# Attention: value products issued in portions of 128 queries, longer planned costs for the filling work, later transfers of the sums

## The chip, the cores and the metric

The kernel runs on one core of a Trainium2 chip. The metric is device time in microseconds. The engines of the core are TensorE (PE, with its weight loads as PEld), VectorE (DVE), ScalarE (ACT), GpSimd (POOL) and SyncE (SP); the last two also issue transfers (DMAs), SP all the loads of operands, POOL those that carry the sums and results of the attention.

## The reference

Four layers follow each other on a sequence of 2048 rows of 640 numbers: attention, state-space convolution, attention, convolution, each on a layer norm of its input and added to it. The change touches the attention alone:

```python
def _A_ref(x, wqkv, wo):
    B, S, D = x.shape                       # 1, 2048, 640
    H, Dh = 32, D // 32                     # 32 heads of 20
    qkv = (x @ wqkv).reshape(B, S, 3, H, Dh).transpose(2, 0, 3, 1, 4)
    q, k, v = qkv[0], qkv[1], qkv[2]
    p = softmax(einsum("bhqd,bhkd->bhqk", q, k) * Dh ** -0.5)
    o = einsum("bhqk,bhkd->bhqd", p, v)
    return o.transpose(0, 2, 1, 3).reshape(B, S, D) @ wo
x = x + _A_ref(layernorm(x), A_wqkv, A_wo)
```

The convolution's kernel is the real part of a sum over 128 modes, `K[d, l] = 2 Re sum_n C[d, n] exp(A[d, n] dt[d] l)`. It does not depend on x, and both convolution layers use the same one.

## The kernel before

**The attention loop.** A layer's 32 heads are taken in 8 groups of 4 (`g`), the 2048 queries in 4 blocks of 512 (`qb`), the keys in 16 tiles of 128 (`kt`), and the four heads of a group in two pairs (`j`). One step of `kt` and `j` is: `scores` multiplies keys and queries (8 matmuls in fp16, line 775, one score group) into one of two PSUM buffers `S`, and ACT takes the exponential of its 128 x 1024 numbers into a tile `pt` (line 778). A layer has 8 x 4 x 16 x 2 = 1024 such steps. After both pairs of a `kt`, `values` multiplies the exponentials with the values (line 792, 8 matmuls in fp32 over 512 queries, which the trace shows as 16 records because each runs in two passes) and sums over `kt` in the PSUM pair `pa`. A row of ones beside the values gives the softmax's denominators.

**The end of a block.** With the last `kt` of a block, DVE copies and adds `pa` into `oc`. The denominators then travel: POOL writes them to DRAM (`sums`: dn<-oc, 4 transfers), reads them back spread over 128 partitions (`load`: dr<-dn), DVE takes the reciprocal (`invert`), POOL writes them (`back`: dn<-dr) and reads them broadcast (`spread`: db<-dn, 4 transfers). At the end of the next block DVE multiplies (`scale`) and POOL stores the block (ot<-oc). The list at line 838 gives the moments, in planned us after the block's end.

**Work that fills TensorE.** Between score groups stands work that later steps need: the projections of queries and keys for the next 128 columns (`qk`, line 560, 15 steps of 8 matmuls for a piece of 512 rows, 8 pieces for a block `b` of columns), the squares of their norms (`norms`, line 488), the projections of values (`values_of`, line 524, 15 matmuls for 128 rows), and in the first layer the convolution's kernel: DVE makes the two factors (tiles `ka`, `kb`), and `contract` (line 314, 16 matmuls a step, two steps for 8 channels) multiplies them. The powers from which DVE starts come by a large load on POOL (kpw<-wd), the finished kernel leaves by kd<-ko.

**What sets the order.** The program is written out by a planner: `plan.pe`, `plan.act` and `plan.dve` are planned clocks, and each piece of work carries a planned cost. `fill`, called after each score group, first places the oldest value product that is ready (`ready`) and then calls `slot` as long as the next step ends 0.5 us before the planned end of the exponential. `slot` takes either a projection step or a `contract` step; `AHEAD` (line 33) says how many us of projections must have been placed by which score group before a `contract` step may go first. `need` forces what a group of heads requires: at `kt` 10 of the last block of a group it places the remaining projections of the next group's columns at once, then `finish` reduces the norms (POOL's k2m), writes the shifts (qm<-mr, 4 transfers), and the loads of the next keys and queries (kop, qop on SP) follow, of which qop<-qm reads the shifts. DVE, POOL's transfers, SP and the matmuls of the loop are tied to the order in which the planner wrote them; other instructions may be moved by the scheduler when they are ready.

`end_jobs`, when all filling work is placed, starts the loads of the output weights (wot), their split on POOL (woh, wol) and, in the first layer, the loads of x (x<-in_x_in). The first tiles of the attention's result are then loaded (otl<-ot) and split on ACT (oh, line 956) between the last exponentials.

Of the kernel before, what the change touches and what calls it, by code (L numbers as in the profile page):

```python
# [21 lines left out]
P = 128  # L22
L = 2048
D = 640
NI = L // P
# [4 lines left out]
NA, NB = 32, 64  # L30
LV = [1.0, 2.0, 4.0, 8.0, 16.0, 32.0, 64.0, 128.0, 256.0, 512.0, 1024.0, 1536.0]
PB = 7
AHEAD = ((0, 0.0), (96, 22.0), (352, 47.0), (478, 72.0), (724, 125.0))
WS = 256.0
LG = 2
BOUND = 30.0
# [4 lines left out]
VP = DH + 1  # L41
VW = VP * 7 + 32
QW = DH * 8
# [38 lines left out]
def mha_s4d_kernel(ctx, tc, x_in, wqkv, wo, lar, aim, cr, ci, ldt, dsk,  # L82
                   c_e1, c_eb, c_f2, c_fa, c_sel, c_lv, c_id, c_sg, c_e16, c_f16, c_id16, out, parts="asas", general=None):
    nc = tc.nc
    plan = Plan()
# [8 lines left out]
    se, te = nc.scalar, nc.tensor  # L94
# [81 lines left out]
    def chain(ins):  # L176
        last[0] = tie(ins, last[0])

    def kgen():
# [124 lines left out]
        def contract(r, bs, sub, ko, a, b):  # L304

            ps = pst("M", [P, 512], F32, tag=f"m{r}", name=f"m{r}")[:, :DC // 4 * NB].rearrange("p (c b) -> p c b", b=NB)
            for c8 in range(DC // 4):
                if c8:
                    yield plan.pe + 0.7, 0.43, True, ()
                plan.on_pe(0.43)  # L310
                for n in range(4):
                    for j in range(4):
                        ch, dd = DC * (sub % 2) + 4 * c8 + j, 4 * c8 + j
                        chain(te.matmul(ps[32 * j:32 * j + 32, c8, :], a[n // 2][:, ch, :], b[n][:, dd, :],  # L314
                                        start=(n == 0), stop=(n == 3), tile_position=(0, 32 * j)))
            evac = lambda: ve.tensor_copy(ko[:, 2 * sub:2 * sub + 2, :], ps)
            emptied(*((None, evac) if r else (evac,)))
            if sub == BC // DC - 1:
                ge.dma_start(kd[bs, :].rearrange("(c j) (a b) -> (j a) c b", j=4, b=NB), ko)
# [49 lines left out]
    part = [None, None]  # L369
# [21 lines left out]
    def attention(x, stats):  # L391
# [121 lines left out]
        def values_of(i, q, ps, w, n):  # L513

            sl = slice(i * P, i * P + P)
            k = 0
            if n == QW:
                plan.on_pe(0.63)
            for ct in range(NCT):
                for a_, m in ((xh, w[0]), (xh, w[1]), (xl, w[0])):  # L520
                    if k == 8 and n == QW:
                        yield 0.0, 0.63, True, ()
                        plan.on_pe(0.63)
                    chain(te.matmul(ps[:, :n], a_[:, ct, sl], m[:, ct, :], start=(k == 0), stop=(k == 14)))  # L524
                    k += 1
            for d in range(n // QW):
                o = Vt[(q + d) % 3][:, i, :VP * 8].rearrange("p (h r) -> p h r", r=VP)[:, :, :DH]
                src = ps[:, d * QW:d * QW + QW].rearrange("p (h r) -> p h r", r=DH)
                if d == 1 or d and i % 2:
                    se.activation(o, src, AF.Copy, scale=1.0 / WS)  # L530
                elif n == QW:
                    evac = lambda: ve.tensor_scalar_mul(o, src, 1.0 / WS)
                    emptied(*((None, evac) if i % 2 else (evac,)))
                else:
                    ve.tensor_scalar_mul(o, src, 1.0 / WS)

        def jobs():
# [40 lines left out]
            def vq(q):  # L578
                make = stage(2 * D + q * QW, QW, "v")
                yield plan.pe + 5.0, 0.0, False, ()  # L580
                w = make()
                t0 = plan.dve
                for i in range(NI):
                    yield t0, 0.63, False, (i % 2,)
                    yield from values_of(i, q, pst("M", [P, 512], F32, tag=f"m{i % 2}", name=f"m{i % 2}"), w, QW)
                have.add(("v", q))

# [35 lines left out]
        def slot(until=None):  # L623

            if head[0] is None:
                head[0] = next(todo[0], None)
            begun = head[0] and head[0][2]
            if pend and part[0] is None and not begun and (head[0] is None or spent[0] >= ahead(len(ends) - 2)):
                t, f, args = pend[0]
                r = free.index(min(free))  # L630
                t = max(t + 0.15, free[r])
                if t <= plan.pe or until is None and head[0] is None:
                    part[:] = f(r, *args), (t, 0.43, True, ())
                    pend.pop(0)
            step = part[1] if part[0] else head[0]
            if step is None:
                return False
            t = max([step[0], *(free[r] for r in step[3])])
            if until and (t > plan.pe or plan.pe + step[1] > until):
                return False  # L640
            plan.on_pe(0.0, t)
            if part[0]:
                part[1] = next(part[0], None)
                if part[1] is None:
                    part[0] = None
            else:
                spent[0] += step[1]
                head[0] = next(todo[0], None)
            return True
# [111 lines left out]
        sums_ = [plan.pe]  # L761
# [19 lines left out]
            ends.append(plan.act)  # L781
            return pt

        def values(qb, g, kt, pts, pa):

            V = Vt[g // 2 % 3]
            plan.on_pe(0.865)
            for r in range(2):
                rows = slice(64 * r, 64 * r + 64)
                for j in range(4):  # L790
                    h = 4 * (g % 2) + j
                    chain(te.matmul(pa[r][32 * j:32 * j + 32, :], V[rows, kt, VP * h:VP * h + 32],  # L792
                                    pts[j // 2][rows, 512 * (j % 2):512 * (j % 2) + 512],
                                    start=(kt == 0), stop=(kt == NI - 1), tile_position=(64 * r, 32 * j)))
            if kt == NI - 1:
                blk = 4 * g + qb
                oc = ev.tile([P, 512], F32, name="oc")
                dr = ev.tile([P, 16], F32, name="dr")
                db = []
                rows = dn[0, blk].rearrange("(j c) f -> j (c f)", j=4)  # L800
                plan.dve = max(plan.dve, plan.pe + 0.25)
                ve.tensor_copy(oc, pa[0])
                ve.tensor_add(oc, oc, pa[1])
                sums_[0] = plan.dve + 0.15
                if scaled:
                    scaled.pop()()

                def sums():
                    for j in range(4):
                        ge.dma_start(rows[j:j + 1, :], oc[32 * j + DH:32 * j + DH + 1, :])  # L810

                def load():
                    ge.dma_start(dr, dn[0, blk])

                def invert():
                    ve.tensor_scalar_max(dr, dr, 1e-30)
                    ve.reciprocal(dr, dr)

                def back():
                    ge.dma_start(dn[1, blk], dr)  # L820

                def spread():
                    rows = dn[1, blk].rearrange("(j c) f -> j (c f)", j=4)
                    db.append(ev.tile([P, 512], F32, bufs=1, name="db"))
                    for j in range(4):
                        ge.dma_start(db[0][32 * j:32 * j + 32, :], rows[j:j + 1, :].to_broadcast([32, 512]))

                def scale():
                    ve.tensor_mul(oc, oc, db[0])
                    later.append((plan.dve + 0.3, store))  # L830
                    later.sort(key=lambda e: e[0])

                def store():
                    for j in range(4):
                        h = 4 * g + j
                        ge.dma_start(ot[h * DH:(h + 1) * DH, 512 * qb:512 * qb + 512], oc[32 * j:32 * j + DH, :])
                later.extend((plan.dve + n, f) for n, f in (
                    (0.2, sums), (5.0, load), (10.0, invert), (11.0, back), (15.5, spread)))
                later.sort(key=lambda e: e[0])
                scaled.append(scale)  # L840

# [22 lines left out]

        def fill(j):

            if ready:
                t = max(ready[0][0] + 0.15, 0.0 if ready[0][3] else sums_[0])
                if t <= plan.pe + 0.1 or j and len(ready) > 2:
                    plan.on_pe(0.0, t)  # L870
                    values(*ready.pop(0)[1:])
            while slot(plan.act - 0.5):
                pass
            drain_later()
            weave()
# [4 lines left out]
        for g in range(H // 4):  # L880
            need((0, 1, 1, 2, 3, 3, 4, 4)[g], ("v", g // 2))
            for qb in range(4):
# [9 lines left out]
                for kt in range(NI):  # L892
                    kc, pts = P * (kt % 8), []
                    for j in range(2):
                        pts.append(scores(kop[j][kt // 8], kc, qop[j][qb % 2]))
                        if j:
                            ready.append((plan.act, qb, g, kt, pts, pa))
                        fill(j)
                    if kt == 2:
                        for j in range(2):  # L900
# [519 lines left out]
```

## Time and profile before

| | us |
|---|---|
| median of 3 runs (2774.07 to 2780.48) | 2777.54 |
| the profiled execution | 2777.71 |
| its span in the profile | 2775.8 |
| ACT busy in the span | 2352.1 |
| PE busy in the span | 2544.2 |
| the exponentials, 2048 of them, ACT busy | 1930.9 |

A row of the profile's groups reads: line, engine, operation, what is written and read, shape, count, then the busy time, the mean ns of one, and the idle time of the engine just before them with what ended it. A row of the time line reads: start and length in us, engine, line, operation, and in brackets the idle time before it and its releaser. The exponentials of the first attention layer run from 111.8 to 1146.2 us of the span, those of the second from 1564.0 to 2545.4 us. Line numbers in these texts are those of the kernel before; line 74 is the helper that records every DVE, POOL and SP operation, so those are told apart by their tiles.

### The profile page before, as it was taken

The page shows a single profiled execution, that of the slowest core. Times are in us where ns is not written, and L with a number is a line of the kernel's source. Part 1 is how long each engine was busy: PE and PEld are TensorE (multiplying, and loading weights), DVE is VectorE, ACT ScalarE, POOL GpSimd, SP SyncE. Part 2 cuts the span into 40 slices and gives each one's busy share as a digit, 9 for nine tenths or more (in the row PEclk, how much of TensorE's full clock was granted, in tenths as well). Part 3 has the DMA queues.
Part 4 walks back from the last instruction along what each step waited for, and adds up shares of the span by engine and source line. Part 5 has one row for each costly group of instructions (what it writes and reads, how often), then busy time and mean ns, then how long its engine had stood idle before and what let it go on. Part 6 is the DMA issues. An engine that isn't in the chain of part 4 may idle for free.

```text
span 2775.8 us, 117573 instructions
## 1 busy us (share of the span) xinstructions
PE 2544.2 (92%) x51968; PEld 1436.6 (52%) x51968; DVE 1469.0 (53%) x3292; ACT 2352.1 (85%) x2781; POOL 821.2 (30%) x1232
## 2 busy tenths in 40 slices
PE   7898989999999997899999998999999888878998
PEld 3453544444444442587796544544444333335988
DVE  8645778978887870366777333332222100002865
ACT  8797989999999998645665698999999999997464
POOL 1112222323223324300573022222322422222376
PEclk9999999999999999999999999999999999999999
DMA  6512232323222223354543112111211211112365
GB/s 230 162 43 68 54 77 52 85 59 78 56 68 55 57 84 96 100 202 179 198 150 92 34 49 66 54 52 51 55 50 38 69 27 38 39 40 71 106 194 159
DMA packets 179128, 238.65 MB, mean 86 GB/s; under 512 B 36144, under 2 KB 124208, under 8 KB 176816
## 3 DMA queue, kind: packets, MB, share of 16 engines
q1 hardware_dynamic: 143168, 184.44, 20.6%
q0 software_dynamic: 35440, 46.58, 7.8%
q8 instruction: 410, 6.72, 1.0%
q14 instruction: 110, 0.90, 0.1%
HBM read 154.87 MB, written 76.03 MB: 83 GB/s over the span
## 4 chain that ended last, share of the span: by engine, by line
ACT 46%; PE 28%; issue 11%; DVE 7%; DMA 6%; POOL 1%; SPq 0%; ACTq 0%; DVEq 0%; POOLq 0%
ACT pt L778 46%; PE pa L792 4%; PE S L775 3%; PE psv L1148 3%; PE po L1054 3%; PE psy L1158 2%; PE psx L1136 2%; PE psx L1113 2%; PE po L1048 1%; DMA kop<-ks 1%; PE m L314 1%; PE pv L524 1%; PE pst L1123 1%; PE m L560 1%; PE pq L681 1%
## 5 line engine op out<-in xcount | busy, mean ns | idle before, releaser
L778 ACT ACTIVATE pt<-S 128x1024 f32<-128x1024 f32 x2048 | 1930.9, 1041 | 71.8 <-PE S L775 57.2
L792 PE MATMUL pa<-pt,V 64*32 64x512 f32 x16384 | 1099.6, 594 | 0.6 <-DVE oc L74 0.6
L775 PE MATMUL S<-qop,kop 61*32 61x512 f16 x16384 | 869.4, 383 | 160.6 <-ACT pt L778 138.0
L775 PEld LDWEIGHTS <-kop 61*32 61x32 f16 x16384 | 369.9, 90 | 830.7 <-issue 726.1
L74 POOL DMA_DIRECT2D dn<-oc x256 | 125.2, 496 | 835.6 <-DVE oc L74 768.2
L792 PEld LDWEIGHTS pa<-pt,V 64*32 64x32 f32 x16384 | 308.9, 107 | 69.4 <-issue 8.3
L74 DVE COPY oc<-pa 128x512 f32<-128x512 f32 x64 | 44.2, 691 | 414.8 <-PE pa L792 414.7
L74 DVE TENSOR_SCALAR qc<-m 128x512 f32<-128x512 f32 x64 | 44.1, 689 | 289.2 <-PE m L560 289.2
L74 POOL DMA_DIRECT2D db<-dn x256 | 129.3, 511 | 139.7 <-DMA dn<-dr 137.0
L74 DVE TENSOR_TENSOR kb<-ktab 128x512 f32<-128x512 f32 x240 | 155.3, 684 | 1.5 <-PE m L314 1.5
L560 PE MATMUL m<-xh,wh 64*32 64x512 f16 x2560 | 139.1, 380 | 3.0 <-DVE qc L74 3.0
L560 PE MATMUL m<-xh,wl 64*32 64x512 f16 x2560 | 138.3, 378 | 0.7 <-issue 0.7
L560 PE MATMUL m<-xl,wh 64*32 64x512 f16 x2560 | 138.4, 378 | 0.0
L74 POOL DMA_DIRECT2D ot<-oc x256 | 130.7, 517 | 8.9 <-DVE oc L74 6.0
L314 PEld LDWEIGHTS m<-kb,ka 128*32 128x32 f32 x5120 | 79.8, 110 | 101.6 <-issue 64.5
L560 PEld LDWEIGHTS <-wh 64*32 64x32 f16 x5120 | 87.7, 94 | 75.4 <-issue 37.6
L1141 POOL TENSOR_TENSOR t<-t,kb 128x512 f32<-128x512 f32 x80 | 102.1, 1276 | 70.3 <-DVE t L74 69.4
L1125 ACT COPY xt<-pst 128x1024 f16<-128x1024 f16 x80 | 81.6, 1023 | 46.7 <-PE pst L1123 46.5
L314 PE MATMUL m<-kb,ka 128*32 128x64 f32 x5120 | 105.8, 224 | 11.4 <-DVE qc L74 11.4
L74 POOL DMA_DIRECT2D dn<-dr x64 | 35.7, 557 | 234.1 <-DVE dr L74 229.8
L1142 POOL TENSOR_TENSOR t<-t,t 128x512 f32<-128x512 f32 x78 | 99.3, 1273 | 7.3 <-DVE t L74 1.3
L970 POOL TENSOR_TENSOR ul<-u,uh 128x640 f16<-128x640 f32 x30 | 46.5, 1566 | 177.7 <-ACT uh L969 177.7
(273 smaller groups left out, 3770.4 us busy)
## 6 DMA issues: line engine op xcount, KB each, us to landing
ka<-kha SPq DMA_DIRECT2D x80, 256.0 KB
kb<-khb SPq DMA_DIRECT2D x80, 256.0 KB
db<-dn POOLq DMA_DIRECT2D x256, 64.0 KB, 2.8
kpw<-wd POOLq DMA_DIRECT2D x20, 576.0 KB, 7.7
qop<-qs SPq DMA_DIRECT2D x256, 40.0 KB
kop<-ks SPq DMA_DIRECT2D x128, 80.0 KB
ot<-oc POOLq DMA_DIRECT2D x256, 40.0 KB, 2.6
otl<-ot SPq DMA_DIRECT2D x32, 320.0 KB
```

What stands on the lines that cost most here:

```text
L74: made = f(out, *a, **k)
L314: chain(te.matmul(ps[32 * j:32 * j + 32, c8, :], a[n // 2][:, ch, :], b[n][:, dd, :], start=(n == 0), stop=(n == 3), tile_position=(0, 32 ...
L560: chain(te.matmul(ps[r][32 * t:32 * t + 32, :], a_[rows, ct, 32 * t:32 * t + 32], m[rows, ct, sl], start=(k == 0), stop=(k == 14), tile_po ...
L775: chain(te.matmul(S[32 * t:32 * t + 32, 512 * r:512 * r + 512], kt_[rows, kc + 32 * t:kc + 32 * t + 32], qt[rows, :], start=True, stop=Tru ...
L778: se.activation(pt, S, AF.Exp, scale=SCALE)
L792: chain(te.matmul(pa[r][32 * j:32 * j + 32, :], V[rows, kt, VP * h:VP * h + 32], pts[j // 2][rows, 512 * (j % 2):512 * (j % 2) + 512], sta ...
L1054: te.matmul(pos[hf], oh[:, ct, :], m[:, ct, 320 * hf:320 * hf + 320], start=False, stop=(ct == NCT - 1 and m is wol))
L1113: te.matmul(ps[:, r, i, :], e1[:, e, s, r, :], m[:, s, bs], start=(n == 0), stop=(n == 2))
L1125: se.copy(xt, pt.rearrange("p k g c -> p k (g c)"))
L1141: ge.tensor_mul(t2, t2, kb)
L1142: (ge if g0 else ve).tensor_add(t1, t1, t2)
L1148: te.matmul(pv[:, g].rearrange("p r i c -> p (r i c)"), t1[:, g * P:g * P + P], fa, start=True, stop=True)
```

## The change

The value products of a `kt` are cut into four portions of 128 queries, each a unit of its own in `ready`. `values` takes the portion's number, starts the sum with the first portion of the first `kt`, and runs the block's end with the last portion of the last. `fill` places portions by two rules: while more than 8 wait they are placed whatever the plan says, and otherwise only if one is ready and ends 0.5 us before the planned end of the exponential; more than three waiting go ahead of the filling work, the others behind it.

The planned cost of a `contract` step goes from 0.43 to 0.56 us; a value projection is cut into three pieces of 5 matmuls planned at 0.4 us (before: pieces of 8 and 7 at 0.63). The moments of the sums' transfers go from 5, 10, 11 and 15.5 to 6, 14, 14.5 and 20 planned us. `AHEAD` gets other numbers.

```diff
-AHEAD = ((0, 0.0), (96, 22.0), (352, 47.0), (478, 72.0), (724, 125.0))
+AHEAD = ((0, 0.0), (84, 20.0), (340, 44.0), (466, 68.0), (730, 122.0))
...
-                    yield plan.pe + 0.7, 0.43, True, ()
-                plan.on_pe(0.43)
+                    yield plan.pe + 0.7, 0.56, True, ()
+                plan.on_pe(0.56)
...
-                plan.on_pe(0.63)
+                plan.on_pe(0.4)
...
-                    if k == 8 and n == QW:
-                        yield 0.0, 0.63, True, ()
-                        plan.on_pe(0.63)
+                    if k % 5 == 0 and k and n == QW:
+                        yield 0.0, 0.4, True, ()
+                        plan.on_pe(0.4)
...
-        def values(qb, g, kt, pts, pa):
+        def values(part, qb, g, kt, pts, pa):
...
-            plan.on_pe(0.865)
+            plan.on_pe(0.217)
...
-                    h = 4 * (g % 2) + j
-                    chain(te.matmul(pa[r][32 * j:32 * j + 32, :], V[rows, kt, VP * h:VP * h + 32],
-                                    pts[j // 2][rows, 512 * (j % 2):512 * (j % 2) + 512],
-                                    start=(kt == 0), stop=(kt == NI - 1), tile_position=(64 * r, 32 * j)))
-            if kt == NI - 1:
+                    h, c0 = 4 * (g % 2) + j, P * part
+                    chain(te.matmul(pa[r][32 * j:32 * j + 32, c0:c0 + P], V[rows, kt, VP * h:VP * h + 32],
+                                    pts[j // 2][rows, 512 * (j % 2) + c0:512 * (j % 2) + c0 + P],
+                                    start=(kt == part == 0), stop=(part == 3 and kt == NI - 1), tile_position=(64 * r, 32 * j)))
+            if part == 3 and kt == NI - 1:
...
-                    (0.2, sums), (5.0, load), (10.0, invert), (11.0, back), (15.5, spread)))
+                    (0.2, sums), (6.0, load), (14.0, invert), (14.5, back), (20.0, spread)))
...
-            if ready:
-                t = max(ready[0][0] + 0.15, 0.0 if ready[0][3] else sums_[0])
-                if t <= plan.pe + 0.1 or j and len(ready) > 2:
-                    plan.on_pe(0.0, t)
-                    values(*ready.pop(0)[1:])
+            def quarter(late):
+                if not ready:
+                    return False
+                t = max(ready[0][0] + 0.15, 0.0 if ready[0][4] else sums_[0])
+                if not late and (t > plan.pe + 0.1 or plan.pe + 0.22 > plan.act - 0.5):
+                    return False
+                plan.on_pe(0.0, t)
+                values(*ready.pop(0)[1:])
+                return True
+            while len(ready) > 8:
+                quarter(True)
+            while len(ready) > 3 and quarter(False):
+                pass
             while slot(plan.act - 0.5):
                 pass
+            while quarter(False):
+                pass
...
-                            ready.append((plan.act, qb, g, kt, pts, pa))
+                            ready.extend((plan.act, n, qb, g, kt, pts, pa) for n in range(4))
```

Three places show what moves. The first is on PE, in the first block of the first attention layer. `S` is the score group's buffer, `pa` the sum of value products, `m` a projection's. The program of before:

```order
L775 MATMUL S<-qop_107,kop_103 32x512
L792 MATMUL pa_1249<-pt,V_92 32x512 x4
L792 MATMUL pa_1250<-pt,V_92 32x512 x4
L775 LDWEIGHTS kop_101
L775 MATMUL S<-qop_105,kop_101 32x512
...
L560 LDWEIGHTS wh
L560 MATMUL m_1290<-xl,wh 32x512
```

The changed program at the same place:

```order
L775 MATMUL S<-qop_107,kop_103 32x512
L792 MATMUL pa_1249<-pt,V_92 32x128 x4
L792 MATMUL pa_1250<-pt,V_92 32x128 x4
...
L775 LDWEIGHTS kop_101
L775 MATMUL S<-qop_105,kop_101 32x512
...
L792 MATMUL pa_1249<-pt,V_92 32x128 x4
L792 MATMUL pa_1250<-pt,V_92 32x128 x4
L560 LDWEIGHTS wh
L560 MATMUL m_1290<-xl,wh 32x512
```

Three portions now stand between the two score groups where the whole product stood (the pair of rows three times), and the fourth behind the second group, ahead of the projections.

The second place is on POOL, at the start of the second group of heads of the first layer. The program of before, from the shifts of the first `need` on:

```order
L74 DMA qm<-mr 6x512 x4
L74 DMA kd<-ko 128x8x64
L74 DMA dn<-oc 16x1x32 x4
L74 DMA ot<-oc 20x512 x4
L74 DMA kpw_166<-wd 128x36x32
L74 DMA dr<-dn 128x16
L74 DMA dn<-dr 128x16
L74 DMA db<-dn 32x512 x4
```

The changed program:

```order
L74 DMA qm<-mr 6x512 x4
L74 DMA db<-dn 32x512 x4
L74 DMA kd<-ko 128x8x64
L74 DMA kpw_166<-wd 128x36x32
L74 DMA dn<-oc 16x1x32 x4
L74 DMA ot<-oc 20x512 x4
L74 DMA dr<-dn 128x16
L74 DMA dn<-dr 128x16
L74 DMA db<-dn 32x512 x4
```

The large load kpw no longer stands between the stores of the sums and the load dr that reads them back; it is ahead of both.

The third place is on POOL, at the end of the sixth group of heads of the first layer, around the last reduction of norms (`ISA k2m`). The program of before:

```order
L74 DMA dn<-oc 16x1x32 x4
L74 DMA ot<-oc 20x512 x4
L74 ISA k2m<-k_21327 128x2
L74 DMA dr<-dn 128x16
L74 DMA kpw_166<-wd 128x36x32
L74 DMA qm<-mr 7x512 x4
L74 DMA dn<-dr 128x16
```

The changed program:

```order
L74 DMA dn<-oc 16x1x32 x4
L74 DMA ot<-oc 20x512 x4
L74 DMA dr<-dn 128x16
L74 DMA kd<-ko 128x8x64
L74 DMA dn<-dr 128x16
L74 DMA kpw_165<-wd 128x36x32
L74 ISA k2m<-k_30411 128x2
L74 DMA qm<-mr 7x512 x4
```

The reduction and the shifts have moved from the block's beginning to behind the block's other transfers; on PE the norm products that feed them move from `kt` 3 to `kt` 10 of that block, where `need` forces them.

More of the change, by code (lines that the diff above doesn't have):

```diff
@@ L583, in vq @@
                 for i in range(NI):
-                    yield t0, 0.63, False, (i % 2,)
+                    yield t0, 0.4, False, (i % 2,)
                     yield from values_of(i, q, pst("M", [P, 512], F32, tag=f"m{i % 2}", name=f"m{i % 2}"), w, QW)
@@ L632, in slot @@
                 if t <= plan.pe or until is None and head[0] is None:
-                    part[:] = f(r, *args), (t, 0.43, True, ())
+                    part[:] = f(r, *args), (t, 0.56, True, ())
                     pend.pop(0)
```

## Prediction

> **What bounds the kernel now.** I read the page first, for its groups of instructions, then the windows of the exponentials' line by group of heads, then the time line around the long waits.
>
> ```profile
> span 2775.8 us, 117573 instructions
> ACT 46%; PE 28%; issue 11%; DVE 7%; DMA 6%; POOL 1%; SPq 0%; ACTq 0%; DVEq 0%; POOLq 0%
> L778 ACT ACTIVATE pt<-S 128x1024 f32<-128x1024 f32 x2048 | 1930.9, 1041 | 71.8 <-PE S L775 57.2
> ```
>
> The chain that ended last runs mostly through ACT, and its largest group are the 2048 exponentials. They are idle for only 71.8 us, 57.2 of them because PE's scores came late. Whatever the change does to the attention, that is about all it can win. Per group of heads (stretch, its length, ACT's busy time and instructions, PE's clock, DMA):
>
> ```profile
> 111.80:243.70 131.90, 120.44 (x129) 0.96 0.24 56
> 243.70:385.90 142.20, 121.59 (x129) 0.94 0.26 63
> 1815.80:1938.00 122.20, 121.09 (x129) 1.00 0.17 47
> 1938.00:2059.70 121.70, 120.84 (x130) 1.00 0.19 51
> 2184.30:2302.30 118.00, 117.97 (x129) 1.00 0.15 42
> ```
>
> The last row is a group without filling work: 128 exponentials in 118.0 us, 0.92 each, ACT never idle. That is the floor. The groups at 1815 and 1938 (filled, second layer) lose 4.2 and 3.7 us against it although no long stall stands in them; the first two of the first layer lose 13.9 and 24.2. So there are two losses: a little at every filled `kt`, and a few long stalls.
>
> **The price of a portion.** Starts on PE in steady state, then around a contraction step, then around seven matmuls of a value projection:
>
> ```profile
> 1001.70 0.41 PE L775 MATMUL S<-qop,kop 61*32 61x512 f16 x8 [0.50 <-ACT pt L778]
> 1001.92 1.05 PE L792 MATMUL pa<-pt,V 64*32 64x512 f32 x16
> 1002.78 0.41 PE L775 MATMUL S<-qop,kop 61*32 61x512 f16 x8
> ...
> 236.59 0.41 PE L775 MATMUL S<-qop,kop 61*32 61x512 f16 x8
> 236.94 0.65 PE L314 MATMUL m<-kb,ka 128*32 128x64 f32 x32
> 237.52 0.41 PE L775 MATMUL S<-qop,kop 61*32 61x512 f16 x8
> ...
> 2071.47 0.40 PE L775 MATMUL S<-qop,kop 61*32 61x512 f16 x8
> 2071.80 0.24 PE L524 MATMUL m<-vh,xl 128*128 128x160 f16 x1
> 2072.39 0.41 PE L775 MATMUL S<-qop,kop 61*32 61x512 f16 x8
> ```
>
> A score group takes 0.22 (1001.70 to 1001.92), the whole value product 0.86, two passes of 0.43. A portion of 128 columns was never run. A quarter of the product is 0.215. The upper end comes from the contraction, the row with the shortest passes: 8 passes of 64 columns last 0.65 with the 0.22 of the last one's latency in it, so (0.65 - 0.22) / 7 = 0.061 a pass, against 0.054 if only columns counted (0.43 x 64 / 512). With 0.007 fixed per pass a portion is 2 x (0.108 + 0.007) = 0.23. I take 0.22, nearer to the lower end, as the first step in that 0.061 includes a start. PE then works 0.02 more per `kt`, 10 us a layer, where it has room.
>
> A contraction step costs 0.58 to the next score group, and the step from scores to it 0.35 where scores to values take 0.22: 0.13 for the change of shape, 0.71 in all. The plan said 0.43 and says 0.56 now. Seven matmuls of a value projection cost 0.33 - 0.22 + 0.59 = 0.70, so five at 0.07 less each cost 0.56, planned at 0.4. Three pieces are 1.68, two were 1.47.
>
> **Term 1, the small losses: -9.9.** From the order of each program I counted what stands between a score group and the next, priced it with these rows (a projection step 0.215, a norm product with both changes of shape 0.44), and summed what goes over 0.92. In the filled groups (six in the first layer, five in the second) this overrun was 65.6 + 54.5 us; it becomes 55.5 + 39.1. Of that, 1.0 before and 3.6 after is one interval, term 3. Without it the drop is 12.7 + 15.4 = 28.1. An overrun is lost only as far as the next interval cannot make it up: the groups at 1815 and 1938 lose 4.2 + 3.7 = 7.9 of an overrun of 22.1, 0.35. 28.1 x 0.35 = 9.9. Bounds: 0 (all was made up) and 28. At 0.23 a portion the drop is 15.0 and the term 5.3.
>
> **Term 2, DVE's waits for the sums: -12.1.** The time line at the second group's start:
>
> ```profile
> 261.38 1.87 POOL L74 DMA_DIRECT2D kpw<-wd  x1
> 263.25 0.56 POOL L74 DMA_DIRECT2D dr<-dn  x1
> 268.95 0.17 DVE L74 TENSOR_SCALAR dr<-dr 128x16 f32<-128x16 f32 x1 [4.57 <-DMA dr<-dn]
> 271.81 0.84 PE L314 MATMUL m<-kb,ka 128*32 128x64 f32 x32 [3.65 <-DVE qc L74]
> 273.35 1.02 ACT L778 ACTIVATE pt<-S 128x1024 f32<-128x1024 f32 x1 [4.03 <-PE S L775]
> 275.48 1.03 ACT L778 ACTIVATE pt<-S 128x1024 f32<-128x1024 f32 x1 [1.11 <-PE S L775]
> ...
> 367.80 0.18 DVE L74 TENSOR_SCALAR dr<-dr 128x16 f32<-128x16 f32 x1 [4.03 <-DMA dr<-dn]
> 372.43 1.02 ACT L778 ACTIVATE pt<-S 128x1024 f32<-128x1024 f32 x1 [5.87 <-PE S L775]
> 374.56 3.08 ACT L778 ACTIVATE pt<-S 128x1024 f32<-128x1024 f32 x3 [1.11 <-PE S L775]
> ```
>
> The load dr is issued behind the large kpw and lands 5.7 us later (263.25 to 268.95). DVE stands at `invert`; the factors kb and the emptying qc are behind it, PE waits for qc, the scores stand behind that, and ACT idles 4.03 and, at the next exponential, 1.11. The same at 372: 5.87 + 1.11. Together 12.1. In the changed order kpw is ahead of the sums in the first place, and in the second `invert` stands 8 exponentials behind dr instead of 1, 7.4 us against the 5.7 the load took. What hides the load then is DVE's work on kb; if the waits reappear at other blocks, the term falls to 0. More than 12.1 is not to be had here: I found no other wait of DVE for dr with a stall of ACT behind it.
>
> **Term 3, a burst: +2.6.** In the last block of the first group `need` now finds a whole piece of 15 projection steps and the norm product (before: two steps and the norm product), as `AHEAD` asks for less there (23.1 us placed instead of 24.1). It overruns by 3.6 instead of 1.0.
>
> **Term 4, a late reduction: +7.5.** The second group starts late today because its shifts come late:
>
> ```profile
> 232.52 0.38 PE L488 MATMUL m<-sq,sel 128*32 128x512 bf16 x1 [0.33 <-DVE sq L74]
> 243.67 1.02 ACT L778 ACTIVATE pt<-S 128x1024 f32<-128x1024 f32 x1 [0.55 <-PE S L775]
> 248.72 0.58 PE L775 MATMUL S<-qop,kop 61*32 61x512 f16 x1 [4.58 <-DMA qop<-qm]
> 250.47 1.03 ACT L778 ACTIVATE pt<-S 128x1024 f32<-128x1024 f32 x1 [5.77 <-PE S L775]
> 252.60 1.03 ACT L778 ACTIVATE pt<-S 128x1024 f32<-128x1024 f32 x1 [1.11 <-PE S L775]
> 254.18 1.03 ACT L778 ACTIVATE pt<-S 128x1024 f32<-128x1024 f32 x1 [0.55 <-PE S L775]
> ...
> 895.06 2.10 ACT L778 ACTIVATE pt<-S 128x1024 f32<-128x1024 f32 x2 [0.46 <-PE S L775]
> ```
>
> From the norm product at 232.5 the chain (reduction, shifts, qm, SP's loads, qop) needs 16 us to the scores at 248.7, and there are 11 exponentials to hide it. ACT idles 0.55 + 5.77 + 1.11 + 0.55 = 8.0. At the seventh group (895.06) it idles 0.46, because its norm product stood 15 exponentials earlier. In the changed order it stands at `kt` 10 too, so that group gets the second group's stall: 8.0 - 0.5 = +7.5. It may be more, as kpw is now queued on POOL just ahead of the reduction, and SP's remaining loads behind qop<-qm: up to 10. If the chain is hidden, 0.
>
> **Term 5, the first output tiles: +2.5.**
>
> ```profile
> 1051.00:1063.00 12.00, 9.98 (x232) 4.12 (x212) 0.00 (x0) 12.00 (x14) 4.07 (x4) 1.00 0.94 348
> 1089.65 0.95 SPq L74 DMA_DIRECT2D otl<-ot  x2
> 1093.16 1.58 ACT L956 CAST oh<-otl 128x640 fp32r<-128x640 f32 x2 [7.43 <-DMA otl<-ot]
> ```
>
> Late in the first layer ACT waits 7.43 for otl. Three loads of x fill the DMA engines for about 12 us (share 0.94) and are long done then. In the changed order they stand on SP straight ahead of otl, 8 exponentials (7.4 us) before oh: 12 + 3.5 for otl (1089.65 to 1093.16) - 7.4 = 8.1 if nothing else waits, about 12 if the store ot has to get through beside them. I take 10: +2.5, from -2 to +5.
>
> The longer times for `back` and `spread` cost nothing: db is needed a block (29.5 us) after the sums, and 20 planned us plus its transfers end before.
>
> **Sum**, on the execution's own 2777.7: -9.9 - 12.1 + 2.6 + 7.5 + 2.5 = -9.4, so **2768**. That execution is within 0.2 us of the median of the runs.
>
> **Rivals.** *Only the waits count (2775).* A portion takes 0.23 and an overrun is made up more often: term 1 is 3 us, and the losses of terms 3 to 5 (12.6) eat term 2: -2.5. For it: all filled groups together lose little outside the stalls. *The waits move (2780).* The new order puts DVE behind another load; in the first layer DVE waits for dr elsewhere, term 2 is 0, and the rest sums to +2.7. *Slower: a fixed price per pass (2807).* Four times as many passes at 0.25 a portion would put 0.14 more on each `kt`. The filled groups hold 111 to 123 us of PE work at 0.22 and would hold 119 to 131, over ACT's 118: PE becomes the bound and loses 72 us there, against 42 (0.35 x 120) lost to overruns now, +29, and the other terms sum to +0.5. It decides from 0.24 a portion. Against it speaks the contraction's 0.061 a pass. The Trainium skill's page TensorEngine Tiling, section Instruction Overhead, says each matmul has about 60 cycles of overhead and warns against splitting a dimension that is already small; read as an addition to every pass, an estimate from it is 0.025 us at 2.4 GHz (its page TensorE: Matmul & The Clock Gate), 0.265 a portion and PE bound. The contraction's passes, 0.007 over their columns, don't show it; no run here has a pass of 128 columns in eight tiles. *Better (2752).* The seventh group's chain is hidden and two thirds of the overrun drop is won: -18.7 - 12.1 + 2.6 + 2.5 = -25.7.
>
> **How the numbers follow.** Chances: the forecast 0.50, with 2758 to 2775 as its own spread; only the waits 0.20; the waits move 0.13; fixed price 0.08; better 0.09. The range leaves out the fixed price and the far part of the better case: 2750 to 2786. About 0.2% (5.5 us) is what a measurement can tell from no change. Faster takes nearly all of the forecast, the better case and a little of the second: 0.60. Same takes the rest of the forecast and most of the second and third: 0.25. Slower: 0.15.
>
> **What would show it.** Right: portions 0.21 to 0.23 apart; no wait of DVE for dr over 2 us in the second group; the group at 1815 nearer 120.5 than 122.2; a stall of about 6 us at the first exponentials of the seventh group of the first layer. Wrong: portions at 0.24 or more with filled groups over 126 us; new waits of PE for qc; or a seventh group as short as today.

## The result and the profile after

The changed kernel takes **3645.6 us** (median of 4 runs, 3634.1 to 3655.3), the kernel before 2778.3: a ratio of 1.312, with a 95% interval from 1.308 to 1.316. The forecast was 2768, its range 2750 to 2786. The profiled execution took 3643.6 us, with a span of 3641.7.

The changed kernel's page first: span; busy time, share and instructions of each engine; the DMA queue that brings instructions (packets, MB, share); the chain that ended last; then groups (busy us, mean ns, idle time before them and what ended most of it).

```profile
span 3641.7 us, 215879 instructions
...
PE 2816.8 (77%) x101120; PEld 2190.2 (60%) x101120; DVE 1466.9 (40%) x3292; ACT 2409.5 (66%) x2781; POOL 819.0 (22%) x1232
...
q8 instruction: 794, 13.01, 1.5%
...
PE 65%; issue 21%; ACT 7%; DVE 3%; DMA 3%; POOL 1%; SPq 0%; ACTq 0%; DVEq 0%; POOLq 0%
...
L778 ACT ACTIVATE pt<-S 128x1024 f32<-128x1024 f32 x2048 | 1988.9, 1024 | 881.2 <-PE S L775 853.5
L792 PE MATMUL pa<-pt,V 64*32 64x128 f32 x65536 | 1501.7, 275 | 457.2 <-issue 454.4
L792 PEld LDWEIGHTS pa<-pt,V 64*32 64x32 f32 x65536 | 1213.2, 107 | 636.6 <-issue 581.8
```

The same lines of the kernel before, as far as they have not been shown:

```profile
PE 2544.2 (92%) x51968; PEld 1436.6 (52%) x51968; DVE 1469.0 (53%) x3292; ACT 2352.1 (85%) x2781; POOL 821.2 (30%) x1232
...
q8 instruction: 410, 6.72, 1.0%
```

The exponentials' idle time has grown from 71.8 to 881.2 us, almost all of it waiting for scores. The chain has changed hands: ACT's share fell from 46% to 7%, PE's rose from 28% to 65%. Yet PE is less busy by share than before, 77% against 92%. Just ahead of the portions it stood 457 us in all, and for 454 of these the releaser is "issue": the profile shows nothing that it waited for. A bound engine that stands idle and waits for no other engine is what has to be explained.

What has nearly doubled is the count of PE's instructions. One f32 matmul of the code leaves four PE records: two weight loads and two passes (32,768 portions' matmuls make 65,536 of each), an f16 one leaves two. The cut adds 2 x (101,120 - 51,968) = 98,304 records. The instruction queue carried 13.01 - 6.72 = 6.29 MB more, 64 bytes for each, in packets of 13.01 MB / 794 = 16.4 KB, 256 instructions.

In the changed kernel's windows (length; then busy us and number of records for PE, PEld, DVE, ACT and POOL; clock, DMA share, GB/s) there are a filled stretch of the first layer and a group of the second layer without filling work:

```profile
1200.00:1300.00 100.00, 74.87 (x3387) 56.33 (x3380) 46.54 (x102) 67.25 (x70) 23.08 (x43) 1.00 0.18 44
2950.80:3102.60 151.80, 111.78 (x5129) 81.88 (x5136) 9.63 (x20) 122.36 (x129) 39.47 (x66) 0.99 0.13 36
```

The kernel before, in the densest of its windows of 100 us and in a group without filling work:

```profile
400.00:500.00 100.00, 99.24 (x2912) 49.16 (x2908) 88.72 (x197) 98.05 (x103) 33.07 (x54) 1.00 0.28 68
2184.30:2302.30 118.00, 95.85 (x2048) 39.76 (x2048) 9.73 (x20) 117.97 (x129) 39.55 (x66) 1.00 0.15 42
```

PE and PEld together: before, 58 records per us in the densest window, 35 in the unfilled group. After, 67.7 in the filled stretch and 67.6 in the unfilled one: the same rate for two different mixes of work. An unfilled group needs 64 key tiles x 160 records (128 for the product, 32 for the two score groups) = 10,240. In ACT's 118.0 us that would be 87 per us. At the filled stretch's 67.7 it takes 151.3, and it took 151.8.

PE's time line in that group of the changed kernel (start, us, line and operation, count, idle time before):

```profile
2997.02 1.14 PE L792 MATMUL pa<-pt,V 64*32 64x128 f32 x64
2997.89 0.48 PE L775 MATMUL S<-qop,kop 61*32 61x512 f16 x8
...
3001.15 0.87 PE L792 MATMUL pa<-pt,V 64*32 64x128 f32 x43
3003.09 0.52 PE L792 MATMUL pa<-pt,V 64*32 64x128 f32 x19 [1.07 <-issue]
```

The first pair is undisturbed: four portions, 64 passes, 0.87 us from their start to the next score group, 0.218 a portion. This is what the prediction took. With the weight loads that is 128 records in 0.87 us, 147 per us, so for that long PE went twice as fast as its mean. The last pair shows where the time goes: a stall of 1.07 us in the middle of a product, after 43 of its 64 passes, where no other engine is awaited. The instruction queue from 2200 to 2300 us, in the second layer of both kernels (packets, MB, share), before:

```profile
q8 instruction: 14, 0.23, 0.9%
```

and after:

```profile
q8 instruction: 27, 0.44, 2.0%
```

Twenty-seven packets in 100 us are one every 3.7 us, with 256 instructions in each: 69 per us.

The trace also holds the time of every packet, and the stalls follow the packets. PE stands for more than 0.3 us with "issue" as the releaser 602 times in the changed kernel, 651 us together, and all 602 of these stalls end 1.1 to 1.8 us after the end of an instruction packet (median 1.39); if they fell anywhere between packets, about a fifth would. The kernel before has two such stalls. No two of the 794 packets overlap: one takes 1.07 us in the median, and two never start closer than 3.24 us.

**The theory**: instructions reach PE at about 68 per us and no faster, and the change asks for more. **The rivals**: the new order and planned times; the short f32 passes with four times the weight loads; a fixed price per pass, as the slower rival of the prediction had it.

### The profile page after: what moved, and what is told of

Same layout as the page of the kernel before. It is cut to its first block, busy times and chain, and to the rows that moved or that the text cites. A ratio compares the mean times of both kernels' runs of the same rounds, so it can differ in the third digit from the quotient of the medians.

```text
span 3641.7 us, 215879 instructions
## 1 busy us (share of the span) xinstructions
PE 2816.8 (77%) x101120; PEld 2190.2 (60%) x101120; DVE 1466.9 (40%) x3292; ACT 2409.5 (66%) x2781; POOL 819.0 (22%) x1232
## 3 DMA queue, kind: packets, MB, share of 16 engines
q8 instruction: 794, 13.01, 1.5%
## 4 chain that ended last, share of the span: by engine, by line
PE 65%; issue 21%; ACT 7%; DVE 3%; DMA 3%; POOL 1%; SPq 0%; ACTq 0%; DVEq 0%; POOLq 0%
PE pa L792 26%; PE S L775 13%; PE m L560 6%; ACT pt L778 6%; PE m L314 3%; PE psv L1158 2%; PE psy L1168 2%; PE m L524 2%; PE po L1064 1%; PE pv L524 1%; PE psx L1146 1%; PE psx L1123 1%; PE pkx L1021 1%; PE pkf L1038 1%; PE pst L1133 1%
## 5 line engine op out<-in xcount | busy, mean ns | idle before, releaser
L778 ACT ACTIVATE pt<-S 128x1024 f32<-128x1024 f32 x2048 | 1988.9, 1024 | 881.2 <-PE S L775 853.5
L792 PE MATMUL pa<-pt,V 64*32 64x128 f32 x65536 | 1501.7, 275 | 457.2 <-issue 454.4
L792 PEld LDWEIGHTS pa<-pt,V 64*32 64x32 f32 x65536 | 1213.2, 107 | 636.6 <-issue 581.8
L775 PE MATMUL S<-qop,kop 61*32 61x512 f16 x16384 | 1061.5, 386 | 209.9 <-issue 99.8
L775 PEld LDWEIGHTS <-kop 61*32 61x32 f16 x16384 | 403.8, 91 | 402.2 <-issue 350.9
L560 PE MATMUL m<-xh,wh 64*32 64x512 f16 x2560 | 188.3, 382 | 20.7 <-issue 20.7
L560 PE MATMUL m<-xl,wh 64*32 64x512 f16 x2560 | 186.3, 380 | 20.8 <-issue 20.8
L560 PE MATMUL m<-xh,wl 64*32 64x512 f16 x2560 | 188.6, 382 | 15.9 <-issue 15.9
L560 PEld LDWEIGHTS <-wh 64*32 64x32 f16 x5120 | 129.1, 93 | 68.6 <-issue 59.7
L74 DVE COPY ko<-m 128x128 f32<-128x128 f32 x80 | 23.2, 290 | 211.2 <-PE m L314 211.0
```

What stands on the lines that cost most here:

```text
L74: made = f(out, *a, **k)
L560: chain(te.matmul(ps[r][32 * t:32 * t + 32, :], a_[rows, ct, 32 * t:32 * t + 32], m[rows, ct, sl], start=(k == 0), stop=(k == 14), tile_po ...
L775: chain(te.matmul(S[32 * t:32 * t + 32, 512 * r:512 * r + 512], kt_[rows, kc + 32 * t:kc + 32 * t + 32], qt[rows, :], start=True, stop=Tru ...
L778: se.activation(pt, S, AF.Exp, scale=SCALE)
L792: chain(te.matmul(pa[r][32 * j:32 * j + 32, c0:c0 + P], V[rows, kt, VP * h:VP * h + 32], pts[j // 2][rows, 512 * (j % 2) + c0:512 * (j % 2 ...
```

## The experiments

**Whole products under all other edits** (e1_whole). The changed kernel with one portion of 512; the new rule's limits are scaled to it (placed anyway when more than 2 wait, otherwise, where they fit, ahead of the filling work):

```diff
-            plan.on_pe(0.217)
+            plan.on_pe(0.865)
...
-                            ready.extend((plan.act, n, qb, g, kt, pts, pa) for n in range(4))
+                            ready.extend((plan.act, n, qb, g, kt, pts, pa) for n in range(1))
...
```

> All of the change except the cut: the product stays whole (512 queries, 0.865 planned), placed by the new rule. If the number of instructions that PE must be supplied with is the bound (the theory), it goes back to that of before, PE no longer waits for nothing, and the time is 2760 to 2785. If the new order, the longer planned steps or the later transfers of the sums cost the time (rival), it stays near 3600.

It took 2830.6 us, 1.0188 of before (1.0173 to 1.0202). The loss of 867 us falls to 55 (against 2776.0, the kernel before beside these runs), so the order and the planned times are not its cause. But the time is 46 us above the end of the range expected: something in the other edits costs time too, and e9_plan below divides it.

**The cut alone** (e2_cut), in the kernel before, in its old order:

```diff
-            for r in range(2):
...
+            for part in range(4):
+                for r in range(2):
...
-                    chain(te.matmul(pa[r][32 * j:32 * j + 32, :], V[rows, kt, VP * h:VP * h + 32],
...
+                        chain(te.matmul(pa[r][32 * j:32 * j + 32, c0:c0 + P], V[rows, kt, VP * h:VP * h + 32],
...
```

> Only the cut: the kernel before with each product as four portions of 128 queries back to back, planned and ordered as before. Same number of PE instructions as in the changed kernel, so supply as the bound gives 3550 to 3700, with about 68 instructions per us on PE in the densest stretches. If the order or the planner's numbers cost the time, 2778. A fixed price per pass as in the prediction's slower rival gives about 2807.

**The scores cut instead** (e5_scores), products whole:

```diff
-            for t in range(4):
...
-                    chain(te.matmul(S[32 * t:32 * t + 32, 512 * r:512 * r + 512],
-                                    kt_[rows, kc + 32 * t:kc + 32 * t + 32], qt[rows, :],
...
+            for part in range(4):
+                for t in range(4):
...
+                        chain(te.matmul(S[32 * t:32 * t + 32, 512 * r + c0:512 * r + c0 + P],
+                                        kt_[rows, kc + 32 * t:kc + 32 * t + 32], qt[rows, c0:c0 + P],
...
```

> The kernel before with its products whole and the scores instead cut in four pieces of 128 queries: 98,304 instructions more on PE, exactly as many as the change adds, all of f16 and with no f32 pass shorter than before. Supply as the bound gives 3550 to 3700 again, whatever the kind of instruction. If it is the f32 portions (their short passes, or four times the f32 weight loads) that cost the time, 2780 to 2900.

e2_cut took 3626.3 us (ratio 1.306, 1.303 to 1.308), e5_scores 3626.8 (1.306, 1.304 to 1.308), two runs of each. Both are as the theory had it, and they agree to 0.5 us. The page of e5_scores:

```profile
PE 2926.7 (81%) x101120; PEld 1925.9 (53%) x101120; DVE 1473.2 (41%) x3292; ACT 2440.9 (67%) x2781; POOL 819.3 (23%) x1232
...
q8 instruction: 794, 13.01, 1.5%
...
L776 PEld LDWEIGHTS <-kop 61*32 61x32 f16 x65536 | 930.7, 91 | 1193.7 <-issue 1095.5
L776 PE MATMUL S<-qop,kop 61*32 61x128 f16 x65536 | 1138.0, 220 | 474.9 <-issue 381.4
L793 PE MATMUL pa<-pt,V 64*32 64x512 f32 x16384 | 1292.2, 605 | 56.4 <-issue 55.1
```

Here the f32 product is as it was, and the short passes are f16. PE's busy time is 110 us more than in the changed kernel and PEld's 264 less, but the number of records, 101,120 of each, and the packets of the instruction queue, 794, are the same, and the time is within 19 us. "Issue" has moved ahead of the scores, to the place of the added instructions. What is paid for is the number of PE's instructions and not their kind; the order and the planned times, which differ between the changed kernel and e2_cut, make 19 us of 867, which the runs hardly separate. From 2400 to 2500 us e5_scores ran 69.0 records per us (3458 + 3442), e2_cut 66.5 (3326 + 3325).

**The cut in two, alone** (e12_half): as e2_cut, with `part` in range(2) and 256 queries.

> The kernel before with each product cut in two back to back: a third of the instructions that the cut in four adds. If supply is a ceiling of about 68 per us, only stretches that go over it pay: the kernel before stood at 49 to 56 per us in the windows from 200 to 1000 us and gets about 17 more, 66 to 73, so 10 to 50 us are lost in all: 2785 to 2830, and groups without filling work stay at 118. If every added instruction or pass costs a fixed time, a third of e2_cut's 850: about 3060.

It took 2869.5 us, 1.033 (1.031 to 1.034): 91 us lost where a third of e2_cut's loss is 283. Two windows of e12_half, a filled group of the first layer and an unfilled one of the second:

```profile
637.00:757.00 120.00, 115.64 (x3914) 68.69 (x3913) 93.66 (x211) 109.38 (x114) 30.46 (x52) 1.00 0.25 58
2380.90:2498.90 118.00, 96.15 (x3072) 56.29 (x3072) 9.63 (x20) 117.94 (x129) 28.31 (x56) 1.00 0.14 36
```

The unfilled group runs 52 records per us and takes 118.0 us as before, with ACT never idle: 17 more per us cost nothing where 33 would have fitted. The filled stretch runs at 65 and passes 114 exponentials in 120 us, where ACT alone would pass 130. So it is a ceiling, not a price. I had put the loss at 10 to 50 us from means over 200 us, and that was too small. A mean hides the bursts (contraction steps and projections) that go over the ceiling inside it; this is shown only in part: PE's stalls for "issue" over 0.3 us come to 37 us in e12_half's trace, against 1.9 before, and I did not trace the rest of the loss.

**Portions of 256 under the whole change** (e3_256):

```diff
-                    h, c0 = 4 * (g % 2) + j, P * part
+                    h, c0 = 4 * (g % 2) + j, 256 * part
...
```

The limits of the new rule are scaled with it, to 4 and 1 waiting in place of 8 and 3.

> The whole change with portions of 256 queries in place of 128. By the ceiling 2790 to 2860, the upper part of it from the rule for placing products. By a fixed price per instruction or pass about 3070.

It took 2861.8 us, 1.030 (1.028 to 1.032), 2 us above the ceiling's end and 208 below the fixed price's. With as many instructions as e12_half it comes out 8 us faster, and in portions of 128 (changed kernel against e2_cut) the rest of the change comes out 19 us slower. The intervals of each pair touch, so neither sign is shown, and both are small beside the supply.

**The later transfers of the sums alone** (e8_sums), on the kernel before:

```diff
-                    (0.2, sums), (5.0, load), (10.0, invert), (11.0, back), (15.5, spread)))
+                    (0.2, sums), (6.0, load), (14.0, invert), (14.5, back), (20.0, spread)))
```

> Only the later transfers of the sums (6, 14, 14.5, 20), on the kernel before. By term 2 of the prediction DVE no longer waits for dr at 269 and 368 and ACT gains 12.1 us: 2766. If the waits move to another load (rival), 2775 to 2781.

It took 2773.8 us, 0.9988 (0.9977 to 0.9999): 2 us, with an interval that all but touches no change. That is 8 us above what term 2 gives and 1 us under the rival's range. Its group of exponentials, then its time line at the second block whose wait term 2 counted and at the third group's start:

```profile
L778 ACT ACTIVATE pt<-S 128x1024 f32<-128x1024 f32 x2048 | 1929.8, 1040 | 71.6 <-PE S L775 57.2
```

```profile
366.99 0.17 DVE L74 TENSOR_SCALAR dr<-dr 128x16 f32<-128x16 f32 x1
...
383.58 1.02 ACT L778 ACTIVATE pt<-S 128x1024 f32<-128x1024 f32 x1 [5.40 <-PE S L775]
385.72 28.22 ACT L778 ACTIVATE pt<-S 128x1024 f32<-128x1024 f32 x29 [1.11 <-PE S L775]
```

DVE no longer waits for dr at 367, and the stall of 5.87 us at 372 in the kernel before is gone. Eleven us later ACT stalls 5.40 at the start of the next group, where PE waits for the shifts (qop); before, that start had 2.15. Counted by group, the exponentials' idle time falls by 9.7 us in the second group and grows by 3.7 in the third, 2.5 in the fourth and 5.0 in the sixth. Over both layers it is 71.6 us against 71.8: the waits moved.

**All of the change's numbers, whole products, the old rule** (e9_plan): `AHEAD`, steps at 0.56, projections in thirds at 0.4, later transfers, without the new `fill` and the cut.

> All of the change's numbers (AHEAD, contraction steps at 0.56, value projections in thirds at 0.4, later transfers of the sums) on the kernel before, with its whole products placed by its own rule. If the 54 us that e1_whole lost come from the new rule for placing products, 2765 to 2785. If they come from the numbers, 2815 to 2840.

It took 2790.8 us, 1.0042 (1.0029 to 1.0055), 6 us above the first range and far below the second. So of e1_whole's 55 us some 12 come from the numbers and the other 43 from the new rule with whole products; the exponentials' idle time shows the latter (132.9 us in e1_whole, 85.8 in e9_plan), spread over many groups, but I did not follow them to a cause. The long stalls of ACT in e9_plan's time line:

```profile
257.93 1.02 ACT L778 ACTIVATE pt<-S 128x1024 f32<-128x1024 f32 x1 [6.33 <-PE S L775]
...
517.78 1.02 ACT L778 ACTIVATE pt<-S 128x1024 f32<-128x1024 f32 x1 [8.79 <-PE S L775]
...
906.11 1.02 ACT L778 ACTIVATE pt<-S 128x1024 f32<-128x1024 f32 x1 [7.86 <-PE S L775]
...
1104.90 0.72 ACT L956 CAST oh<-otl 128x640 fp32r<-128x640 f32 x1 [3.13 <-DMA otl<-ot]
```

The stall at 906, the seventh group's start, is the one of term 4. The one at 518, the fourth group's start, no term had.

**The next group's inputs asked for earlier** (e13_need8), on e8_sums:

```diff
-                    if qb == 3 and kt == 10 and g + 1 < H // 4:
+                    if qb == 3 and kt == 8 and g + 1 < H // 4:
```

> e8_sums with the next group's inputs asked for at key tile 8 of a group's last block in place of 10. The chain from the norm product to the first scores took 16 us with 11 exponentials to hide it; four more hide 3.7 us of it at the three or four group starts of the first layer that stall for 3 to 6 us: 2758 to 2767. If the norm product's own inputs are what is late, no change, 2774; if the earlier burst on PE costs as much, 2770 to 2780.

It took 2766.5 us, 0.9960 (0.9946 to 0.9974): faster than both kernels, 12 us under before. The exponentials of e13_need8:

```profile
L778 ACT ACTIVATE pt<-S 128x1024 f32<-128x1024 f32 x2048 | 1928.4, 1040 | 60.5 <-PE S L775 46.2
```

Their idle time falls from 71.6 to 60.5 us: 11 us, inside the 7 to 16 that the expectation asked for. It falls in the second, third, sixth and tenth groups, by 7.4, 4.9, 4.2 and 6.7 us, whose starts stalled in e8_sums. But the seventh group gets 7.0 us more, with a new stall at its start where PE waits for qop, and the tenth group lies in the second layer, which the expectation did not count. So the sum came out as expected and not every part of it, which is in part luck.

## Why the prediction was wrong

**The step that failed** is the price of a portion, and with it term 1. The prediction said of the cut: "PE then works 0.02 more per `kt`, 10 us a layer, where it has room." The duration of an undisturbed portion was right: 0.218 us, forecast 0.22. What was wrong is that a duration is all it costs. The cut leaves columns nearly as they were and multiplies the product's instructions by four; the sum had no term for how many instructions PE can be supplied with. The trace of before could not show the ceiling as such, since no 100 us of it hold more than 59 records per us. But it showed two edges. One is that rate, and the prediction bounded the portion's duration by the nearest row; done here too, this gives an estimate: at 58 per us a key tile's 160 records take 2.76 us in place of 1.84, over 1024 key tiles 940 us. With nothing as the lower end, the range would have reached to about 3720, and held the result. The other is that two instruction packets never start closer than 3.33 us there, which is 77 instructions per us, where an unfilled group of the changed kernel asks for 87.

**The overrun of term 1** could then not fall: the filled groups no longer follow ACT's 0.92 (the seventh takes 185.6 us, 1.45 for each exponential).

**The slower rival** (a fixed price per pass, 2807) had the direction but not the mechanism. It would decide from 0.24 a portion, and an undisturbed portion takes 0.218. Of the signs of being wrong, filled groups over 126 us came, without portions that last 0.24. The Trainium skill's page TensorEngine Tiling (Array Packing), section Instruction Overhead, on which it drew, gives each matmul about 60 cycles; passes of 128 columns in eight tiles do not show that as an addition, as 64 of them take 0.87 us with their columns, where the prediction's estimate from the page, 0.265 a portion, gives 1.06. Its advice not to take a tiling factor from a dimension that is already small is not tested here.

**Term 2** (-12.1): right where it was read and wrong in what is late next. The changed kernel's `invert` stands without a wait in the second group, and in e8_sums the stalls at 273 and 372 are gone (about 1.1 us of each remain). But ACT keeps 71.6 of 71.8 us, as the chain behind the shifts (qop) stalls instead. The rival "the waits move" named DVE and dr for it. It was mostly PE and qop, but in the sixth group of e8_sums it was also that: DVE waits 3.99 us for dr at 882, and ACT stalls 2.41 behind it.

**Term 4** (+7.5): right in kind in e9_plan, where the same numbers work without the cut, and somewhat small: the seventh group's start has a stall of 7.86 us and 2.9 more behind it, 10.8 in all, where before had 0.46. The term's upper end was 10. The changed kernel has only 1.18 and 1.62 there. Its exponentials come every 1.45 us in that group, so the 11 that stand behind the norm product cover 16 us, as long as the chain took before (an estimate). The fourth group's start (8.79) was missed: I looked for that mechanism only where the norm product moved in the rows I had read.

**Term 3** (+2.6): right in e1_whole, which has the burst as priced, 15 projection steps and then the norm product. ACT's stall behind it is 6.31 us, before 3.08.

**Term 5** (+2.5): not settled. In the changed kernel ACT stands 8.06 us ahead of the first oh, 0.6 more than before. The profile names no releaser; otl is issued only 5.1 us before the end of this stall, 11.6 us behind the loads of x, which is the order that the term counted on. But this kernel runs at another pace. With whole products ACT waits less there than before: 3.13 and 1.19 in e9_plan, 1.91 in e1_whole.

All numbers together cost 12 us with whole products, where terms 2 to 5 summed to +0.5.

## What to carry to other kernels

- Count instructions per engine and us as a resource, beside busy time. Before work is cut into smaller pieces, divide the new count by the time it must fit, and compare it with the densest stretch the trace has shown; above that, the price is unknown and the range must say so.
- An f32 matmul counts four here, an f16 one two. Where an engine is idle, waits for "issue", and its records per us are the same in stretches of different work, look at the instruction queue.
- A wait that is removed is worth only the distance to the next late one: total the idle time of the bound engine before and after, not the wait.

## What the runs showed of the hardware

- PE ran 66 to 69 records per us in the windows shown of the three kernels with 98,304 records more, and 71 in the densest 100 us found (the changed kernel from 2797 us, 3572 + 3570). Its instructions come in packets of 16.4 KB, 256 instructions, in the changed kernel 3.79 us apart in the median and never under 3.24. The kind of instruction made no difference: 98,304 more f16 records and 98,304 more f32 records gave 3626.8 and 3626.3 us.
- The queue is not short of bandwidth by its share: it took 1.5% of the DMA engines' time in the changed kernel. A packet's own transfer took 1.07 us in the median, no second one was under way, and PE's stalls ended 1.1 to 1.8 us after one had ended. What fills the rest of the time from one packet to the next was not measured.
- Below the ceiling added instructions were free: 52 per us in place of 35 left a group at 118.0 us. In a short burst (128 records in 0.87 us) PE went at 147 per us.
